# A dynamic convolution followed by a maxout layer: three pairs of taps of columns 24 to 27 added on VectorE, GpSimd's gate as a transfer, sums in three parts, the last copy shared

## The chip, the cores and the metric

The kernel runs on one core of a Trainium2 chip. The metric is the device time of one execution in microseconds, as the median over several executions. In the text TensorE (PE in the profile) does the matrix products, VectorE (DVE) and ScalarE (ACT) the elementwise work, GpSimd (POOL) and SyncE (SP) issue most of the transfers.

## The reference

```python
w = softmax(weight_gen, axis=-1)            # (8, 4160, 8 heads, 7 taps)
x_pad = x with 6 zero rows ahead of each sequence
y[b, s, h, :] = sum over k of w[b, s, h, k] * x_pad[b, s + k, h, :]      # 24 channels a head, 192 in all
g = maximum(y @ w1, y @ w2)                 # 192 -> 1024
out = g @ w_out                             # 1024 -> 192
```

There are 8·4160 = 33280 tokens. The maximum is computed as h1 + relu(h2 − h1): the matrix w2 − w1 makes the "hidden" products, ScalarE applies ReLU to them, and the part h1 @ w_out is the product of y with w1 @ w_out (the tile `w10`).

## The kernel before, in words

**Columns and batches.** Each of the 128 partitions holds 260 consecutive tokens; token c of every partition is "column" c. Columns are worked on in batches of 16 (the last two have 12 and 8). Batches 0 and 1 are split into units of four columns, the others into units of eight. A unit's first column is written (b, o): batch and offset, so (1, 8) holds columns 24 to 27; it is unit 6, counted from 0.

**VectorE per batch.** `mul` (L198, the instruction at L211) multiplies x with the weights for all seven taps, into `m_t`. `adds` (L217) then sums the taps: L227 adds taps 3 to 5 to taps 0 to 2 in one instruction, L233 adds tap 1 to tap 0 and tap 6 to tap 2, L236 adds those two into `y_t`. Between the three additions, `adds` calls a function `beside(i, 3)` for i = 0, 1, 2; it is how other VectorE work is put between them. In the main loop the first half of a batch has there the three parts of `shift` (L177: the logarithm of the sum is subtracted from the weights' exponents), the second half has `red` (L168: the sum over the taps of the exponentials), in two parts, both ahead of L233.

**The softmax on ScalarE.** For batch b the steps are X.b (the exponential, L153), the sums by VectorE (`red`), l.b (the logarithm, L172, one instruction for the whole batch), `shift` on VectorE, and W.b.o (the exponential again, which makes the weights that `mul` takes, L191). Where X, l and W stand in ScalarE's queue of the main loop is given by the table `SOFTMAX_AT`: the key (g, place) is a group of the main loop and a place in it (0: before the group's last ReLU, 1: after the group's results have been copied out). l.5 stands at (16, 1), l.10 at (44, 1). VectorE's work for batches b + 1 to b + 3 is issued by `extra` (L762), called for every tile of batch b; so the sums of batch 5 are issued by the tile with offset 8 of batch 2 and those of batch 10 by the tile with offset 13 of batch 7, which lie in the groups 16 and 44.

**TensorE.** y must be turned for the products. In the opening (units 0 to 7) TensorE does it and adds the taps at the same time: `sum_transpose` (L270, steps y.u; its products at L281) multiplies each tap's block of `m_t` with an identity matrix and accumulates all seven taps in PSUM: 6 blocks · 7 taps · 2 halves = 84 products of 64 columns per unit. From unit 8 on the taps are added on VectorE, and the turned block `yt` comes from a transposing transfer (`transpose`, L241; the transfer at L245 on SyncE's queue).

**The main loop.** A tile is a chunk of hidden products. From group 8 on, a group has three tiles, held in PSUM as `hda`, `hdb`, `hdc`, each with one buffer. In `hidden` (L495) TensorE makes the hidden products of the first two tiles (L336), the first half of the results of earlier columns (`out_first`, L388 and L376, into `op_ps`, one buffer), the third tile's hidden products, and the second half of the results (`out_second`). ScalarE does the three ReLUs (L346) and copies the results out of `op_ps` (`evac`, L434). Before `out_second` TensorE waits for a signal that ScalarE passes on behind the first two ReLUs (`relay`). VectorE's steps of a group (`beside`) are issued before its l step. The tile with number 16 + 3k opens group 8 + k; tile 208 is the first of a unit of batch 13.

**The gate.** `transpose` ends by letting GpSimd copy one column of `yt` into a small tile `gate` (L253). The copy waits for the transposing transfer; the loads of x and of `weight_gen` that GpSimd issues behind it (x for the next batch or the one after it, `weight_gen` for three batches later) start only then.

**The opening.** It is written out as a string of steps, each step being name.arguments: m.b.o is `mul`, n.b `red`, s.b `shift`, y.u `sum_transpose`, e.u the copy of its result into `yt`, h and r hidden products and ReLU, A, B, D, E the parts of the results. The step named `a` calls `adds(b, o, first=True)`, which stops after L227; no step of the string uses it.

**The end.** `evac` has a branch for the very last pair of columns: ScalarE copies both from PSUM into `o_last` (L422), and ScalarE and SyncE issue one transfer each.

Of the kernel before, what the change touches and what calls it, by code (L numbers as in the profile page):

```python
# [9 lines left out]
FP32 = mybir.dt.float32  # L10
BF16 = mybir.dt.bfloat16
# [12 lines left out]
def kernel(  # L24
# [18 lines left out]
    HF = F // 2  # L43
# [8 lines left out]
    NB = len(BATCHES)  # L52
# [27 lines left out]
    consts = ctx.enter_context(tc.tile_pool(name="consts", bufs=1))  # L80
# [83 lines left out]
    def red(b, i=0, of=1):  # L164
        if i == 0:
            s_ts[b] = psm.tile([P, BATCHES[b][1] * H], FP32, name="sum_t", tag="sum")
        hs, at, ap = part(b, i, of)
        nc.vector.reduce_sum(out=s_ts[b][:, hs], in_=_sub(e_ts[b], at, ap), axis=AX.X)  # L168
# [48 lines left out]
    def adds(b, o, first=False, beside=lambda i, of: None):  # L217


        w = dict(pieces(b))[o]  # L220
        n = w * D

        def taps(at, step, cnt):
            return _sub(m_t, K * o * D + at * n, [[step * n, cnt], [1, w * D]])

        beside(0, 3)
        nc.vector.tensor_tensor(out=taps(0, 1, 3), in0=taps(0, 1, 3), in1=taps(3, 1, 3), op=ALU.add)  # L227
        if first:
            return
        beside(1, 3)  # L230
        if b not in y_ts:
            y_ts[b] = py.tile([P, 16 * D], BF16, name="y_t", tag="y")
        nc.vector.tensor_tensor(out=taps(0, 2, 2), in0=taps(0, 2, 2), in1=taps(1, 5, 2), op=ALU.add)  # L233
        beside(2, 3)

        nc.vector.tensor_tensor(  # L236
            out=_sub(y_ts[b], o * D, [[64, 2], [P, 3 * w // 2], [1, 64]]),
            in0=taps(0, 1, 1), in1=taps(2, 1, 1), op=ALU.add,
        )

    def transpose(u):  # L241

        b, o, n = UNITS[u]
        yt = pyt.tile([P, 8 // 2 * 3 * P], BF16, name="yt", tag="yt")
        nc.sync.dma_start_transpose(  # L245
            out=yt[:, 0:n // 2 * 3 * P].rearrange("p (b t) -> p b t", t=P),
            in_=y_ts[b][:, o * D:(o + n) * D],
        )
        yt_ts[u] = yt
        while held:  # L250
            held.pop(0)()

        nc.gpsimd.tensor_copy(out=gate, in_=yt[:, 0:1])  # L253
# [11 lines left out]
        return slice(64 * j, 64 * j + 64)  # L265


    LEFT = (0, 1, 2, K - 1)

    def sum_transpose(u, i=None):  # L270

        b, o, n = UNITS[u]
        assert n == 4
        to = "h" if i == 0 else "o"
        yps = yps_of[u, i] = ps[to].tile([P, 1024], FP32, name="yps", tag="hd" if i == 0 else "op")
        ks = range(6) if i is None else range(3 * i, 3 * i + 3)
        for k in ks:
            for t in range(K):
                at = K * o * D + (t * 6 + k if i is None else (K * i + t) * 3 + k % 3) * P
                for r in range(2):  # L280
                    nc.tensor.matmul(  # L281
                        yps[:, r * 512 + k * 64:r * 512 + (k + 1) * 64],
                        lhsT=m_t[half(r), at:at + P], rhs=ident[half(r), half(r)],
                        start=(k == ks[0] and t == 0), stop=(t == K - 1),
                        skip_group_check=True,
                    )
# [129 lines left out]
    def evac(p, n):  # L416

        tile_, at = op_at[p]
        o = o_t[0]
        if p == NT // 2 - 1:  # L420

            nc.scalar.copy(out=_sub(o_last, 0, [[D, 2], [1, D]]),  # L422
                           in_=_sub(tile_, at, [[512, 2], [1, D]]))
            for j, eng in enumerate((nc.scalar, nc.sync)):
                eng.dma_start(
                    out=bass.AP(tensor=out.tensor, offset=dcol(place(p)[0] + 2 * j) * D, ap=[[CPP * D, P], [1, D]]),
                    in_=o_last[:, j * D:(j + 1) * D],
                )
            return
        runs = [[q for q in range(p, p + n) if column(2 * q)[0] == u]  # L430
                for u in range(column(2 * p)[0], column(2 * (p + n - 1))[0] + 1)]
        for qs in runs:
            c, h = place(qs[0])
            copied = nc.scalar.copy(out=_sub(o, c % 24 * D, [[D, len(qs)], [h * D, 2], [1, D]]),  # L434
                           in_=_sub(tile_, at + (qs[0] - p) * D, [[D, len(qs)], [512, 2], [1, D]]))
# [106 lines left out]
    around = consts.tile([P, 2 * P], BF16, name="around")  # L542
    ident, swap = around[:, 0:P], around[:, 64:64 + P]
    zeros = consts.tile([P, PAD * D], BF16, name="zeros")
    gate = consts.tile([P, 1], FP32, name="gate")
    o_last = consts.tile([P, 2 * D], FP32, name="o_last")

    pstage = ctx.enter_context(ExitStack())
    stage = pstage.enter_context(tc.tile_pool(name="pstage", bufs=1))
# [13 lines left out]
    def load_w(h, wi):  # L563

        wsrc = (moe_w1, moe_w2)[wi]
        return nc.sync.dma_start(
            out=ws["E", wi][:, h * HF:(h + 1) * HF],
            in_=bass.AP(tensor=wsrc.tensor, offset=h * HF, ap=[[F, P], [1, HF]]),
        )

    def load_last(h, wi):

        wsrc = (moe_w1, moe_w2)[wi]
        return nc.sync.dma_start(  # L574
            out=ws["T", wi][half(h), :],
            in_=bass.AP(tensor=wsrc.tensor, offset=P * F + h * HF, ap=[[F, 64], [1, HF]]),
        )
# [124 lines left out]
    def results_buffer(_):  # L702
# [22 lines left out]
        e.0.1 d.0 d.2 t.0 k.3 t.2 T.3 d.1 T.4 h.0 h.1 t.1 X.1 r.0 lx.0.8.4 T.1 lo.0 r.1 m.0.4 n.1 v.0 h.2  # L725
        lx.1.0.8 V.1 y.1 r.2 l.1 h.3 e.1 m.0.8 lg.2@l.1 s.1 V.0 m.0.12 r.3 h.4 W.1.0 m.1.0 y.2 h.5 r.4 p.0
        e.2 r.5 h.6 lx.1.8.8@r.4 lg.3@e.2 y.3 W.1.8 h.7 lh.2 C.1 C.0 C.2 A.3 W.1.4 X.2 r.6 e.3 B.3 m.1.4 h.8
        D.3 y.4 r.7 r.8 Z.0 E.3 n.2 X.3 l.2 m.1.8 A.4 e.4 W.1.12 lx.2.0.8.0@r.7 B.4 h.9 D.4 h.10 r.9 E.4 s.2
        r.10 lg.4@r.9 y.5 W.2.0 A.5 h.11 B.5 h.12 e.5 D.5 n.3 r.11 r.12 A.6 m.1.12 E.5 h.13 B.6 D.6 y.6 r.13
        E.6 h.14 e.6 l.3 lx.2.8.8@r.13 h.15 r.14 A.7 W.2.8 B.7 y.7 D.7 r.15 e.7 E.7  # L730
    """

    make_identity(nc, ident_f)
# [28 lines left out]
    def extra(t):  # L762

        u, k = TILES[t]
        b, o, n = UNITS[u]
        s = o + k

        if s == 0 and b + 1 < NB:
            mul(b + 1, 0)
        later = 0 if b < 4 else 5  # L770
        if s == later and b + 1 < NB:

            c = b + 1
# [51 lines left out]
```

## Time and profile before

| | |
|---|---|
| median of 3 executions | 406.01 us (405.65 to 406.52) |
| the profiled execution | 405.37 us |
| its span, first to last instruction | 403.6 us |
| TensorE's granted clock | 1.00 |
| products of the turning in the opening, L281 | 672, 11.4 us busy |
| L253, the gate | 30, 1332 ns on average |
| L168, the sums | 31, 19.7 us busy |
| L422, the last copy | 1, 479 ns |

A line of the timeline has: start, duration (both us), engine, line of the code, operation, output<-input, shapes, count, and in brackets the idle time of the engine before it and what ended it. In the chain of waits a line has: start, duration, engine, output, line, count. A line of the list of waits has: who waited, for whom, us in total, times, the longest. In the groups, "x27 | 155.4, 5754 | 0.0" means 27 instructions, 155.4 us busy, 5754 ns each, and idle time before them. Consecutive instructions of one engine overlap a little in these records: the next one starts before the one ahead is shown to end.

### The profile page before, as it was taken

Reading aid. Unit: us, or ns where it says so; the run is one execution under the profiler, and the core shown is the slowest. Engines: PE = TensorE matmul, PEld = TensorE weight load, DVE = VectorE, ACT = ScalarE, POOL = GpSimd, SP = SyncE. Lnnn points to the kernel's source line nnn. Section 1 sums busy time; section 2 is a strip of 40 time slices with the busy share of each in tenths; the row PEclk is TensorE's granted clock in tenths of the full one; section 3 lists DMA queues with packets and bytes.
Section 4 is the critical chain, followed back from the end, with each engine's and each line's share of the span. In section 5 each row is a group of like instructions: output and inputs, shape, how many; then the busy total and the mean of one; then the engine's idle time right before and its main releaser. Section 6 shows DMA issues by size and latency. Waiting matters only on the chain.

```text
span 403.6 us, 16321 instructions
## 1 busy us (share of the span) xinstructions
PE 394.8 (98%) x7499; PEld 321.3 (80%) x7499; DVE 369.1 (91%) x211; ACT 360.9 (89%) x466; POOL 72.3 (18%) x96
## 2 busy tenths in 40 slices
PE   7799999999999999999999999999999999999996
PEld 3589999777778777778777778877777877787996
DVE  5999999999999999999999999999999999998200
ACT  5999899999999989999899999989999899888872
POOL 3111031211122210222220122122012121200000
PEclk9999999999999999999999999999999999999999
DMA  8956468767768646864766667777457847558304
GB/s 262 222 140 151 120 124 167 183 164 133 190 110 222 182 79 129 240 187 80 217 187 107 141 192 193 99 215 198 81 115 228 178 80 200 141 106 193 104 31 169
DMA packets 60883, 63.16 MB, mean 157 GB/s; under 512 B 47641, under 2 KB 48665, under 8 KB 60816
## 3 DMA queue, kind: packets, MB, share of 16 engines
q1 hardware_dynamic: 52816, 40.15, 36.4%
q0 software_dynamic: 7856, 21.89, 27.4%
q8 instruction: 58, 0.95, 1.0%
q10 hardware_dynamic: 144, 0.10, 0.1%
q14 instruction: 9, 0.07, 0.1%
HBM read 36.55 MB, written 25.56 MB: 154 GB/s over the span
## 4 chain that ended last, share of the span: by engine, by line
PE 92%; ACT 5%; DMA 1%; SPq 1%; issue 0%
PE op_ps L376 42%; PE hdc L336 13%; PE hdb L336 13%; PE hda L336 13%; PE op_ps L388 8%; ACT rd_t L346 2%; DMA ws0E<-in_moe_w_dram 1%; PE hdp L336 1%; PE yps L281 1%; ACT en_t L191 1%; ACT yt L293 1%; ACT e_t L153 0%; ACT w1t L644 0%; SPq L574 0%; ACT w L622 0%
## 5 line engine op out<-in xcount | busy, mean ns | idle before, releaser
L376 PE MATMUL op_ps<-wo,rd_t 64*128 64x192 bf16 x4160 | 210.6, 243 | 0.0
L376 PEld LDWEIGHTS <-rd_t 64*128 64x128 bf16 x4160 | 181.0, 94 | 14.7
L211 DVE TENSOR_TENSOR m_t<-xb,en_t 128x10752 bf16<-128x10752 bf16 (+2 forms) x39 | 187.8, 4821 | 1.5 <-ACT en_t L191 1.4
L336 PEld LDWEIGHTS <-wd 64*128 64x128 bf16 x1824 | 96.8, 94 | 40.4 <-issue 2.5
L346 ACT ACTIVATE rd_t<-hdc 128x1024 bf16<-128x1024 f32 x82 | 84.1, 1025 | 17.8 <-PE hdc L336 16.2
L253 POOL CAST gate<-yt 128x1 f32<-128x1 bf16 x30 | 39.9, 1332 | 271.3 <-DMA yt<-y_t 271.3
L346 ACT ACTIVATE rd_t<-hda 128x1024 bf16<-128x1024 f32 x81 | 83.4, 1030 | 0.2 <-ACT o_t L434 0.2
L346 ACT ACTIVATE rd_t<-hdb 128x1024 bf16<-128x1024 f32 x81 | 83.5, 1031 | 0.0
L227 DVE TENSOR_TENSOR m_t<-m_t 128x4608 bf16<-128x4608 bf16 (+1 forms) x30 | 73.0, 2433 | 0.1
L336 PE MATMUL hdc<-yt,wd 64*128 64x512 bf16 (+1 forms) x552 | 67.9, 353 | 0.0
L434 ACT COPY o_t<-op_ps 128x384 f32<-128x384 f32 (+1 forms) x99 | 56.1, 577 | 12.4 <-PE op_ps L376 12.3
L336 PE MATMUL hdb<-yt,wd 64*128 64x512 bf16 (+1 forms) x540 | 67.1, 355 | 0.0
L336 PE MATMUL hda<-yt,wd 64*128 64x512 bf16 (+1 forms) x540 | 67.1, 355 | 0.0
L388 PE MATMUL op_ps<-w,yt 64*128 64x192 bf16 x780 | 55.5, 243 | 0.0
L388 PEld LDWEIGHTS <-yt 64*128 64x128 bf16 x780 | 39.0, 94 | 14.5 <-issue 0.3
L233 DVE TENSOR_TENSOR m_t<-m_t 128x3072 bf16<-128x3072 bf16 (+1 forms) x30 | 50.2, 1674 | 0.1
L191 ACT ACTIVATE en_t<-wg_t 128x896 bf16<-128x896 f32 (+3 forms) x48 | 35.7, 773 | 3.0 <-PE op_ps L376 2.0
L236 DVE TENSOR_TENSOR y_t<-m_t 128x1536 bf16<-128x1536 bf16 (+1 forms) x30 | 27.5, 916 | 0.6
L177 DVE TENSOR_TENSOR wg_t<-wg_t,sum_t 128x280 f32<-128x280 f32 (+6 forms) x46 | 22.2, 483 | 0.0
L168 DVE TENSOR_REDUCE sum_t<-e_t 128x64 f32<-128x448 f32 (+3 forms) x31 | 19.7, 639 | 2.3 <-ACT e_t L153 2.3
L125 POOL DMA_DIRECT2D xb<-in_x_dram x34 | 18.2, 537 | 17.3 <-ACT rd_t L346 11.0
L153 ACT ACTIVATE e_t<-wg_t 128x896 f32<-128x896 f32 (+2 forms) x18 | 15.9, 886 | 2.1 <-DMA wg_t<-in_weight_gen_dram 2.1
(40 smaller groups left out, 110.0 us busy)
## 6 DMA issues: line engine op xcount, KB each, us to landing
out_dram<-o_t SPq DMA_DIRECT2D x21, 768.0 KB, 4.3
xb<-in_x_dram POOLq DMA_DIRECT2D x30, 384.0 KB, 5.0
out_dram<-o_t SPq DMA_DIRECT2D x22, 384.0 KB, 3.7
wg_t<-in_weight_gen_dram POOLq DMA_DIRECT2D x13, 448.0 KB, 5.7
xb<-xb POOLq DMA_DIRECT2D x7, 288.0 KB, 5.1
wg_t<-in_weight_gen_dram SPq DMA_DIRECT2D x2, 448.0 KB, 5.2
xb<-in_x_dram POOLq DMA_DIRECT2D x4, 192.0 KB, 6.4
xs<-in_x_dram SPq DMA_DIRECT2D x1, 576.0 KB, 4.3
```

Source lines behind the costliest of these rows:

```text
L177: nc.vector.tensor_tensor(out=w_t, in0=w_t, in1=_sub(s_ts[b], hs.start, [[1, hs.stop - hs.start], [0, K]]), op=ALU.subtract)
L191: act = nc.scalar.activation(out=_sub(en_ts[b], (o * WGC + ((i or 0) * J + j) * N * K) * 2, [[2 * N, K], [2, N], [1, 2]]), in_=_sub(wg_ts[ ...
L211: return nc.vector.tensor_tensor(out=m_out, in0=x_in, in1=_sub(en_ts[b], at * H * 2, [[2, K * n * H], [0, G // 2], [1, 2]]), op=ALU.mult,)
L227: nc.vector.tensor_tensor(out=taps(0, 1, 3), in0=taps(0, 1, 3), in1=taps(3, 1, 3), op=ALU.add)
L233: nc.vector.tensor_tensor(out=taps(0, 2, 2), in0=taps(0, 2, 2), in1=taps(1, 5, 2), op=ALU.add)
L236: nc.vector.tensor_tensor(out=_sub(y_ts[b], o * D, [[64, 2], [P, 3 * w // 2], [1, 64]]), in0=taps(0, 1, 1), in1=taps(2, 1, 1), op=ALU.add,)
L253: nc.gpsimd.tensor_copy(out=gate, in_=yt[:, 0:1])
L336: nc.tensor.matmul(hid_out(t, f, j), lhsT=wd_at(j, s, f // 4, f % 4 * P, P), rhs=_sub(yt_ts[u][half(j), :], (s + j) % 3 * P, [[3 * P, w // ...
L346: relu_of[t0] = nc.scalar.activation(out=rd[:, k * 1024:(k + n) * 1024], in_=hd[:, at:at + n * 1024], func=AF.Relu)
L376: return nc.tensor.matmul(op_out(c), lhsT=rd[rows, k * 1024 + at:k * 1024 + at + P], rhs=wo[rows, f * D:(f + 1) * D], start=False, stop=(r ...
L388: nc.tensor.matmul(op_out(c + j), lhsT=yt_ts[u][half(j), (3 * i + (s + j) % 3) * P:(3 * i + (s + j) % 3 + 1) * P], rhs=w10[half(j), s * D: ...
L434: copied = nc.scalar.copy(out=_sub(o, c % 24 * D, [[D, len(qs)], [h * D, 2], [1, D]]), in_=_sub(tile_, at + (qs[0] - p) * D, [[D, len(qs)] ...
```

## The change

- The opening gets the step a.1.8 behind m.1.8: VectorE adds taps 3 to 5 of unit (1, 8) to its taps 0 to 2. `sum_transpose` then accumulates four taps for this unit (0, 1, 2 and 6) where it took seven.
- The gate is a transfer of two elements, issued by GpSimd, where it was a copy by GpSimd.
- `red` in the second half of a batch comes in three parts, the third between L233 and L236.
- The last pair of columns is copied by ScalarE and VectorE, one column each, into two tiles; ScalarE and SyncE issue the transfers as before.
- `load_w` and `load_last` get a case and an argument that no step uses.

```diff
         nc.vector.tensor_tensor(out=taps(0, 1, 3), in0=taps(0, 1, 3), in1=taps(3, 1, 3), op=ALU.add)
         if first:
+            fewer.add((b, o))
             return
...
-        nc.gpsimd.tensor_copy(out=gate, in_=yt[:, 0:1])
+        nc.gpsimd.dma_start(out=gate, in_=yt[0:1, 0:2])
...
-    LEFT = (0, 1, 2, K - 1)
+    fewer = set()
...
+        taps = (0, 1, 2, K - 1) if (b, o) in fewer else range(K)
         for k in ks:
-            for t in range(K):
+            for t in taps:
...
-            nc.scalar.copy(out=_sub(o_last, 0, [[D, 2], [1, D]]),
-                           in_=_sub(tile_, at, [[512, 2], [1, D]]))
-            for j, eng in enumerate((nc.scalar, nc.sync)):
+            for j, (eng, copy) in enumerate(((nc.scalar, nc.scalar.copy), (nc.sync, nc.vector.tensor_copy))):
+                copy(out=o_last[j], in_=tile_[:, at + 512 * j:at + 512 * j + D])
                 eng.dma_start(
                     out=bass.AP(tensor=out.tensor, offset=dcol(place(p)[0] + 2 * j) * D, ap=[[CPP * D, P], [1, D]]),
-                    in_=o_last[:, j * D:(j + 1) * D],
+                    in_=o_last[j],
                 )
...
-    gate = consts.tile([P, 1], FP32, name="gate")
-    o_last = consts.tile([P, 2 * D], FP32, name="o_last")
+    gate = consts.tile([1, 2], BF16, name="gate")
+    o_last = [consts.tile([P, D], FP32, name=f"o_last{j}") for j in range(2)]
...
-        D.3 y.4 r.7 r.8 Z.0 E.3 n.2 X.3 l.2 m.1.8 A.4 e.4 W.1.12 lx.2.0.8.0@r.7 B.4 h.9 D.4 h.10 r.9 E.4 s.2
+        D.3 y.4 r.7 r.8 Z.0 E.3 n.2 X.3 l.2 m.1.8 a.1.8 A.4 e.4 W.1.12 lx.2.0.8.0@r.7 B.4 h.9 D.4 h.10 r.9
+        E.4 s.2 ...
...
-            adds(b + 1, 8, beside=lambda i, of: red(b + 3, i, 2) if b + 3 < NB and i < 2 else None)
+            adds(b + 1, 8, beside=lambda i, of: red(b + 3, i, 3) if b + 3 < NB else None)
```

More of the change, by code (lines that the diff above doesn't have):

```diff
@@ L565, in load_w, with load_last @@
         wsrc = (moe_w1, moe_w2)[wi]
+        at, w = (0, F) if h == 2 else (h * HF, HF)
         return nc.sync.dma_start(
-            out=ws["E", wi][:, h * HF:(h + 1) * HF],
-            in_=bass.AP(tensor=wsrc.tensor, offset=h * HF, ap=[[F, P], [1, HF]]),
+            out=ws["E", wi][:, at:at + w],
+            in_=bass.AP(tensor=wsrc.tensor, offset=at, ap=[[F, P], [1, w]]),
         )
-    def load_last(h, wi):
+    def load_last(h, wi, act=0):
         wsrc = (moe_w1, moe_w2)[wi]
-        return nc.sync.dma_start(
+        return (nc.scalar if act else nc.sync).dma_start(
             out=ws["T", wi][half(h), :],
@@ L727 @@
         e.2 r.5 h.6 lx.1.8.8@r.4 lg.3@e.2 y.3 W.1.8 h.7 lh.2 C.1 C.0 C.2 A.3 W.1.4 X.2 r.6 e.3 B.3 m.1.4 h.8
-        D.3 y.4 r.7 r.8 Z.0 E.3 n.2 X.3 l.2 m.1.8 A.4 e.4 W.1.12 lx.2.0.8.0@r.7 B.4 h.9 D.4 h.10 r.9 E.4 s.2
-        r.10 lg.4@r.9 y.5 W.2.0 A.5 h.11 B.5 h.12 e.5 D.5 n.3 r.11 r.12 A.6 m.1.12 E.5 h.13 B.6 D.6 y.6 r.13
-        E.6 h.14 e.6 l.3 lx.2.8.8@r.13 h.15 r.14 A.7 W.2.8 B.7 y.7 D.7 r.15 e.7 E.7
+        D.3 y.4 r.7 r.8 Z.0 E.3 n.2 X.3 l.2 m.1.8 a.1.8 A.4 e.4 W.1.12 lx.2.0.8.0@r.7 B.4 h.9 D.4 h.10 r.9
+        E.4 s.2 r.10 lg.4@r.9 y.5 W.2.0 A.5 h.11 B.5 h.12 e.5 D.5 n.3 r.11 r.12 A.6 m.1.12 E.5 h.13 B.6 D.6
+        y.6 r.13 E.6 h.14 e.6 l.3 lx.2.8.8@r.13 h.15 r.14 A.7 W.2.8 B.7 y.7 D.7 r.15 e.7 E.7
     """
```

## The prediction

> **What bounds the kernel now.** I read the page first, then the chain of waits, then the timeline engine by engine, and last each place where ScalarE or TensorE takes something that VectorE has made.
>
> ```profile
> span 403.6 us, 16321 instructions
> PE 394.8 (98%) x7499; PEld 321.3 (80%) x7499; DVE 369.1 (91%) x211; ACT 360.9 (89%) x466; POOL 72.3 (18%) x96
> ...
> 41.97 1.22 PE yps L281 x84
> 43.19 1.31 PE hdp L336 x24
> ```
>
> The profiled execution took 405.37 us, 1.8 more than its span, against a median of 406.01; I work out a difference on the span and add it to the median. TensorE is the bound: it is busy 98% of the span, and its pieces of the chain follow without a gap (the products at 41.97 end at 43.19, where the next begin). A microsecond taken from TensorE is therefore won, as long as ScalarE and VectorE can be earlier too. VectorE is the one to doubt:
>
> ```profile
> 31.32 2.95 DVE L211 TENSOR_TENSOR m_t<-xb,en_t 128x5376 bf16<-128x5376 bf16 x1
> 34.19 1.08 DVE L177 TENSOR_TENSOR wg_t<-wg_t,sum_t 128x896 f32<-128x896 f32 x1
> ...
> DVE m_t L211 <- ACT en_t L191: 1.4, 1, 1.4
> ```
>
> The third line is VectorE's only wait after the opening (the list of waits has it once, at 364 us). Between 34 and 357 us VectorE runs without a pause, so whatever is put in at 34 us moves everything behind it by the full amount.
>
> **The columns 24 to 27.** The four remaining taps need 6·4·2 = 48 products where seven needed 84. The 84 took 1.22 us, so the 36 that go are worth 36/84·1.22 = **0.52 us of TensorE**. Nothing hides them; but the gain lasts only while nobody makes TensorE wait later.
>
> On VectorE the new addition is of 128x2304 elements and stands behind the multiplication m.1.8 whose result it reads. The same two forms, in the same dependence, stand near the end:
>
> ```profile
> 357.13 2.96 DVE L211 TENSOR_TENSOR m_t<-xb,en_t 128x5376 bf16<-128x5376 bf16 x1
> 360.12 1.36 DVE L227 TENSOR_TENSOR m_t<-m_t 128x2304 bf16<-128x2304 bf16 x1
> ...
> 36.90 1.09 ACT L191 ACTIVATE en_t<-wg_t 128x896 bf16<-128x896 f32 x1
> ```
>
> There the addition began 2.99 us after the multiplication; before, the next instruction (independent) began 34.19 − 31.32 = 2.87 after it. So a.1.8 begins at 34.31, and an independent successor begins about 0.08 before the end of 1.36 (as 34.19 lies 0.08 before 31.32 + 2.95), at 35.59: **VectorE is 1.40 us later from there on** (1.28 without the dependence, at least). The first taker, the weights W.2.0 on ScalarE (36.90), needs s.2, which then ends at 35.59 + 1.08 = 36.67: covered, by 0.2 us (without that cover ScalarE would be late by the difference, less than what l.5 brings below). The products of y.6 at 41.97 have over 6 us.
>
> **The sums in three parts.** What each part costs is read from the starts:
>
> ```profile
> 80.20 0.61 DVE L168 TENSOR_REDUCE sum_t<-e_t 128x64 f32<-128x448 f32 x1
> 80.73 2.55 DVE L227 TENSOR_TENSOR m_t<-m_t 128x4608 bf16<-128x4608 bf16 x1
> 83.20 0.62 DVE L168 TENSOR_REDUCE sum_t<-e_t 128x64 f32<-128x448 f32 x1
> 83.72 1.75 DVE L233 TENSOR_TENSOR m_t<-m_t 128x3072 bf16<-128x3072 bf16 x1
> 85.51 0.96 DVE L236 TENSOR_TENSOR y_t<-m_t 128x1536 bf16<-128x1536 bf16 x1
> ...
> 95.24 1.75 DVE L233 TENSOR_TENSOR m_t<-m_t 128x3072 bf16<-128x3072 bf16 x1
> 96.91 0.50 DVE L177 TENSOR_TENSOR wg_t<-wg_t,sum_t 128x336 f32<-128x336 f32 x1
> ...
> 316.87 0.50 DVE L168 TENSOR_REDUCE sum_t<-e_t 128x48 f32<-128x336 f32 x1
> 317.28 2.56 DVE L227 TENSOR_TENSOR m_t<-m_t 128x4608 bf16<-128x4608 bf16 x1
> ```
>
> A sum over 448 elements takes 0.53 from start to start, over 336 it takes 0.41; so 280 take 0.35. L236 waits for L233 and begins 1.79 behind it, but an instruction that is independent begins 1.67 behind (96.91). The third sum therefore fills 0.12 us that were empty. Two parts: 0.53 + 0.53 + 1.79 = 2.85; three parts (280, 280, 336): 0.35 + 0.35 + 1.67 + 0.41 = 2.78. That is **0.07 us less per batch**, 0.9 over 13 batches, off a VectorE that doesn't set the end. [...]
>
> What counts is when the sums are complete. The logarithm l.5 of batch 5 reads all of them, and the last third now comes behind L233, the second addition. In the block above: 80.20 + 0.35 + 2.47 (L227) + 0.35 + 1.67 = 85.04, and 0.50 for itself: 85.54, where now it is 83.82. With VectorE's delay at this place, 1.40 less the 0.07 that batch 4 has saved, it is **86.87**. And l.5 isn't moved:
>
> ```profile
> 83.94 0.80 ACT L434 COPY o_t<-op_ps 128x768 f32<-128x768 f32 x1
> 84.64 0.31 ACT L172 ACTIVATE sum_t<-sum_t 128x128 f32<-128x128 f32 x1
> 84.85 1.02 ACT L346 ACTIVATE rd_t<-hda 128x1024 bf16<-128x1024 f32 x1
> 85.75 1.03 ACT L346 ACTIVATE rd_t<-hdb 128x1024 bf16<-128x1024 f32 x1
> 86.75 1.02 ACT L346 ACTIVATE rd_t<-hdc 128x1024 bf16<-128x1024 f32 x1
> 87.67 0.47 ACT L434 COPY o_t<-op_ps 128x384 f32<-128x384 f32 x1
> ...
> 87.19 0.83 PE L336 MATMUL hda<-yt,wd 64*128 64x512 bf16 x6
> ...
> 88.48 0.43 PE L388 MATMUL op_ps<-w,yt 64*128 64x192 bf16 x6
> ```
>
> How fast such a signal is, the opening shows:
>
> ```profile
> 4.72 1.15 DVE L168 TENSOR_REDUCE sum_t<-e_t 128x64 f32<-128x448 f32 x2 [2.28 <-ACT e_t L153]
> ...
> 5.38 0.26 ACT L172 ACTIVATE sum_t<-sum_t 128x64 f32<-128x64 f32 x1 [0.22 <-DVE sum_t L168]
> ```
>
> The first sum (0.62) ends at 5.34, the logarithm begins 0.04 later. So ScalarE would reach l.5 at 84.64 − 0.52 = 84.12 and stand until 86.91: a wait of 2.8 us that doesn't exist now. Queued behind it are the three ReLUs and the copy of group 17. From the start of l.5: 0.21 to the first ReLU, 0.91, 0.91 and 0.92 to the copy, 0.47 for the copy, 0.05 to release TensorE: 3.47 us, so 90.38. TensorE needs that copy at 88.48, since op_ps has one buffer in this phase. It begins at 90.38, **1.90 us later than before**. The other takers are less late: the hidden products at 87.19 need the first ReLU, ready at 88.2, so 1.0. The 0.52 gained are swallowed in this wait, as VectorE, not TensorE, sets when l.5 runs.
>
> The same pattern comes once more at l.10:
>
> ```profile
> 198.53 0.61 DVE L168 TENSOR_REDUCE sum_t<-e_t 128x64 f32<-128x448 f32 x1
> ...
> 203.25 0.31 ACT L172 ACTIVATE sum_t<-sum_t 128x128 f32<-128x128 f32 x1
> ...
> 207.14 0.43 PE L388 MATMUL op_ps<-w,yt 64*128 64x192 bf16 x6
> ```
>
> The sums end at 198.53 + 5.34 + 1.40 − 6·0.07 = 204.85. By itself this would cost 204.89 + 3.47 − 207.14 = 1.22 us. But ScalarE is 1.90 later by then and reaches l.10 at 205.15: no wait. VectorE runs on its own clock, so such delays do not add; the largest counts.
>
> **The gate.** Now the gate's copy waits out VectorE's multiplication:
>
> ```profile
> 74.53 5.75 DVE L211 TENSOR_TENSOR m_t<-xb,en_t 128x10752 bf16<-128x10752 bf16 x1
> 78.60 1.73 POOL L253 CAST gate<-yt 128x1 f32<-128x1 bf16 x1 [8.96 <-DMA yt<-y_t]
> 80.27 0.53 POOL L125 DMA_DIRECT2D xb<-in_x_dram  x1
> ...
> L211 DVE TENSOR_TENSOR m_t<-xb,en_t 128x10752 bf16<-128x10752 bf16 x27 | 155.4, 5754 | 0.0
> ```
>
> It lasts until the multiplication ends. A transfer in its place costs GpSimd one issue, 0.53 like the row below it; at worst it stays at 1.73. The loads behind it start 1.2 us earlier at this place, and are used a batch (24 us) later: 0 on the path either way. VectorE gains nothing: with the copy waiting beside it this multiplication took 5.75 us, as the 27 of its form did on average.
>
> **The last copy.** One ScalarE copy of 384 elements becomes two of 192, side by side.
>
> ```profile
> L434 ACT COPY o_t<-op_ps 128x384 f32<-128x384 f32 x69 | 31.9, 478 | 3.5 <-PE op_ps L376 3.5
> ...
> L434 ACT COPY o_t<-op_ps 128x768 f32<-128x768 f32 x30 | 24.1, 805 | 8.9 <-PE op_ps L376 8.9
> ```
>
> (805 − 478)/384 = 0.85 ns an element, so 192 take 478 − 163 = 315 ns: **−0.16 us**, fully at the end. VectorE's copy out of PSUM isn't in the trace; VectorE is idle there, and between 0.2 and 0.4 us for it the gain is 0.08 to 0.16.
>
> **Sum:** +1.90 − 0.16 = +1.74; 406.01 + 1.74 = **407.7 us**. With the delay at 1.28 instead of 1.40, or 0.25 more in ScalarE's string, +1.6 to +2.0.
>
> **Rivals.**
> *The wait is hidden.* If TensorE can do without ScalarE for the time of the wait, it keeps its 0.52 and the end its 0.16: −0.7, 405.3 us. For it: now the sums end at 83.82, l.5 begins 0.82 later, and the copy that TensorE needs at 88.48 ends at 88.14; both places have room. It decides if the sums end by 84.45 (84.49 + 3.47 is 88.48 − 0.52); even with no delay of VectorE's the third part would end at 85.54. 12%.
> *The delays add.* If ScalarE's stand makes VectorE late as well (by its weights), l.10 costs its 1.22 + 0.52 again: +3.5, 409.5 us. The point is where weights come later than the multiplication that takes them. Against it: the list has VectorE waiting for ScalarE's weights just once, at the end. 12%.
> *A turned block becomes the limit instead.* With l.5 harmless, the next thinnest place is the block of tile 208:
>
> ```profile
> 316.04 0.96 POOL L253 CAST gate<-yt 128x1 f32<-128x1 bf16 x1 [9.85 <-DMA yt<-y_t]
> ...
> 317.49 0.83 PE L336 MATMUL hda<-yt,wd 64*128 64x512 bf16 x6
> ```
>
> It has landed 1.45 us ahead of its use; TensorE 0.52 earlier and VectorE 0.6 later leave 0.3. A landing 0.6 us slower would take half of the gain: 405.7 us. 6%.
>
> **How the numbers follow.** The forecast has 70%, by itself 407.2 to 408.4. Slower by over 0.2% (0.8 us, about what a measurement of this kernel can tell from no change): forecast and adding delays, 82%. The hidden wait lies at −0.17%, so its 12% are split, 5 faster and 7 same; with the 6 of the block that is 13% same. The range runs from 405.9 to 408.9: it leaves out the hidden wait and half of the adding one, 18%.
>
> **What would show it.** The list of waits must have ScalarE's sum_t waiting for VectorE's sum_t once for some 2.8 us, at 84 us, and no second time over 0.3; TensorE must have about 2.4 us of gaps between 86 and 91 and none after; y.6 must take 0.70; VectorE's shift s.2 must begin at 35.6. I am wrong if ScalarE passes l.5 without that wait, or if it waits and TensorE runs on.

## The result, and the profile after

| | before | after |
|---|---|---|
| median (range), 6 executions each | 405.70 us (405.50 to 406.52) | 407.25 us (407.01 to 407.83) |
| ratio after / before, with its interval | | 1.0042 [1.0030, 1.0054] |
| the profiled execution, its span | 405.37 us, 403.6 us | 407.56 us, 405.8 us |

The change makes the kernel about 1.6 us slower. In the profile after, lines behind the edits have moved by one or two: `op_ps` is now L378 and L390 (they were L376 and L388), the hidden products are L338 (L336), `evac` is L435 (L434), the gate L254 (L253), the additions L234 and L237 (L233 and L236). First the head of the page and the rows that answer to the opening:

```profile
span 405.8 us, 16275 instructions
```

```profile
31.71 2.95 DVE L211 TENSOR_TENSOR m_t<-xb,en_t 128x5376 bf16<-128x5376 bf16 x1
...
34.69 1.36 DVE L227 TENSOR_TENSOR m_t<-m_t 128x2304 bf16<-128x2304 bf16 x1
...
35.97 1.08 DVE L177 TENSOR_TENSOR wg_t<-wg_t,sum_t 128x896 f32<-128x896 f32 x1
...
42.17 0.88 PE L283 MATMUL yps<-around,m_t 64*128 64x64 bf16 x48
42.87 1.49 PE L338 MATMUL hdp<-yt,wd 64*128 64x256 bf16 x24
```

The multiplication m.1.8 starts at 31.71, 0.39 later than before (31.32), though nothing ahead of it was changed; other profiled executions start earlier or later too, so where a time of this profile is held against one of before, the 0.39 is named or taken off. The shift that began 34.19 − 31.32 = 2.87 us behind m.1.8 now begins 4.26 behind it: VectorE is 1.39 us later. The products of y.6 take 42.87 − 42.17 = 0.70 us instead of 1.22.

The timeline where batch 5's sums are completed, VectorE and ScalarE, then TensorE:

```profile
81.92 0.43 DVE L168 TENSOR_REDUCE sum_t<-e_t 128x40 f32<-128x280 f32 x1
...
82.27 2.54 DVE L227 TENSOR_TENSOR m_t<-m_t 128x4608 bf16<-128x4608 bf16 x1
...
84.74 0.43 DVE L168 TENSOR_REDUCE sum_t<-e_t 128x40 f32<-128x280 f32 x1
...
85.09 1.75 DVE L234 TENSOR_TENSOR m_t<-m_t 128x3072 bf16<-128x3072 bf16 x1
...
86.76 0.49 DVE L168 TENSOR_REDUCE sum_t<-e_t 128x48 f32<-128x336 f32 x1
87.17 0.94 DVE L237 TENSOR_TENSOR y_t<-m_t 128x1536 bf16<-128x1536 bf16 x1
87.28 0.31 ACT L172 ACTIVATE sum_t<-sum_t 128x128 f32<-128x128 f32 x1 [2.68 <-DVE sum_t L168]
...
90.21 0.49 ACT L435 COPY o_t<-op_ps 128x384 f32<-128x384 f32 x1
```

```profile
85.75 0.83 PE L338 MATMUL hdc<-yt,wd 64*128 64x512 bf16 x6
...
87.47 0.83 PE L378 MATMUL op_ps<-wo,rd_t 64*128 64x192 bf16 x16 [0.90 <-ACTq L411]
...
88.55 0.82 PE L338 MATMUL hda<-yt,wd 64*128 64x512 bf16 x6 [0.25 <-ACT rd_t L348]
...
89.47 0.82 PE L338 MATMUL hdb<-yt,wd 64*128 64x512 bf16 x6
...
90.75 0.42 PE L390 MATMUL op_ps<-w,yt 64*128 64x192 bf16 x6 [0.46 <-ACT o_t L435]
```

ScalarE stands for 2.68 us until VectorE's third sum has ended at 87.25. TensorE is 0.13 us earlier than before when it reaches this place (85.75 against 85.88: the late opening and the 0.52 gained) and 2.27 us later when it leaves it (90.75 against 88.48): 2.40 us lost between five neighbouring steps, at four stops. The first stop, at 87.47, waits for the relay (the `ACTq L411` in the bracket), which stands behind l.5 in ScalarE's queue. The brackets show less, since the rows of products overlap (before, a row of 0.83 us where the next begins 0.65 behind it); starts are the safer reading: before, these steps came 0.65, 0.66, 0.65 and 0.64 us apart, now 1.72, 1.08, 0.92 and 1.28. From there to the end TensorE loses and wins nothing more: its last products begin 2.26 us later (400.12 against 397.86), and the span is 405.8 − 403.6 = 2.2 us longer.

The list of waits has ScalarE waiting for a sum once more, for 0.2 us, and nothing else of the kind:

```profile
DVE o_last L425 <- ACT o_last L425: 24.1, 1, 24.1
...
DVE m_t L211 <- ACT en_t L191: 3.0, 2, 2.8
...
ACT sum_t L172 <- DVE sum_t L168: 2.9, 2, 2.7
```

The second line is VectorE waiting for ScalarE's weights. That wait, at 364 us before, has grown from 1.4 to 2.8 us, because ScalarE is later there by more than VectorE is; no product of TensorE is later for it. The first line is the tail, which didn't go as forecast:

```profile
401.70 0.48 ACT L435 COPY o_t<-op_ps 128x384 f32<-128x384 f32 x1 [0.82 <-PE op_ps L378]
402.31 0.32 ACT L425 COPY o_last<-op_ps 128x192 f32<-128x192 f32 x1
...
402.66 0.36 DVE L425 COPY o_last<-op_ps 128x192 f32<-128x192 f32 x1 [24.14 <-ACT o_last L425]
403.05 0.34 SPq L426 DMA_DIRECT2D out_dram<-o_last  x1
```

VectorE's half of the last copy waits for ScalarE's half and starts when that has ended. Both read the same PSUM tile, `op_ps`, in which TensorE has summed the products.

### The profile page after: what moved, and what is told of

The parts are those of the page before. It is cut to its first block, busy times and chain, and to the rows that moved or that the text cites. A ratio compares the mean times of both kernels' runs of the same rounds, so it can differ in the third digit from the quotient of the medians.

```text
span 405.8 us, 16275 instructions
## 1 busy us (share of the span) xinstructions
PE 395.7 (98%) x7463; PEld 320.4 (79%) x7463; DVE 370.3 (91%) x226; ACT 360.6 (89%) x466; POOL 49.2 (12%) x96
## 4 chain that ended last, share of the span: by engine, by line
PE 79%; DVE 13%; ACT 5%; DMA 1%; issue 1%; SPq 0%; DVEq 0%; ACTq 0%
PE op_ps L378 37%; PE hdc L338 11%; PE hdb L338 11%; PE hda L338 11%; PE op_ps L390 7%; DVE m_t L211 6%; DVE m_t L227 2%; ACT rd_t L348 2%; DVE m_t L234 2%; DMA xs<-in_x_dram 1%; PE yps L283 1%; DVE y_t L237 1%; DVE sum_t L168 1%; PE hdp L338 1%; DVE wg_t L177 0%
## 5 line engine op out<-in xcount | busy, mean ns | idle before, releaser
L378 PE MATMUL op_ps<-wo,rd_t 64*128 64x192 bf16 x4160 | 210.5, 243 | 0.9 <-ACTq L411 0.9
L378 PEld LDWEIGHTS <-rd_t 64*128 64x128 bf16 x4160 | 180.7, 94 | 16.0 <-ACTq L411 1.4
L211 DVE TENSOR_TENSOR m_t<-xb,en_t 128x10752 bf16<-128x10752 bf16 (+2 forms) x39 | 187.5, 4814 | 3.0 <-ACT en_t L191 3.0
L338 PEld LDWEIGHTS <-wd 64*128 64x128 bf16 x1824 | 96.4, 94 | 41.1 <-issue 2.9
L227 DVE TENSOR_TENSOR m_t<-m_t 128x4608 bf16<-128x4608 bf16 (+1 forms) x31 | 74.1, 2392 | 0.1
L338 PE MATMUL hdc<-yt,wd 64*128 64x512 bf16 (+1 forms) x552 | 67.9, 353 | 0.0
L338 PE MATMUL hda<-yt,wd 64*128 64x512 bf16 (+1 forms) x540 | 67.0, 355 | 0.2 <-ACT rd_t L348 0.2
L435 ACT COPY o_t<-op_ps 128x384 f32<-128x384 f32 (+1 forms) x99 | 56.1, 578 | 12.4 <-PE op_ps L378 12.4
L338 PE MATMUL hdb<-yt,wd 64*128 64x512 bf16 (+1 forms) x540 | 67.0, 355 | 0.1
L390 PE MATMUL op_ps<-w,yt 64*128 64x192 bf16 x780 | 55.5, 243 | 0.5 <-ACT o_t L435 0.5
L254 POOL DMA_DIRECT2D gate<-yt x30 | 15.3, 512 | 298.9 <-DMA yt<-y_t 298.9
L390 PEld LDWEIGHTS <-yt 64*128 64x128 bf16 x780 | 38.8, 94 | 15.3 <-issue 1.0
L234 DVE TENSOR_TENSOR m_t<-m_t 128x3072 bf16<-128x3072 bf16 (+1 forms) x30 | 50.0, 1667 | 0.1
L237 DVE TENSOR_TENSOR y_t<-m_t 128x1536 bf16<-128x1536 bf16 (+1 forms) x30 | 27.2, 906 | 0.1
L168 DVE TENSOR_REDUCE sum_t<-e_t 128x40 f32<-128x280 f32 (+6 forms) x44 | 21.3, 486 | 2.3 <-ACT e_t L153 2.3
```

The lines of the kernel that those rows point to most:

```text
L211: return nc.vector.tensor_tensor(out=m_out, in0=x_in, in1=_sub(en_ts[b], at * H * 2, [[2, K * n * H], [0, G // 2], [1, 2]]), op=ALU.mult,)
L237: nc.vector.tensor_tensor(out=_sub(y_ts[b], o * D, [[64, 2], [P, 3 * w // 2], [1, 64]]), in0=taps(0, 1, 1), in1=taps(2, 1, 1), op=ALU.add,)
L338: nc.tensor.matmul(hid_out(t, f, j), lhsT=wd_at(j, s, f // 4, f % 4 * P, P), rhs=_sub(yt_ts[u][half(j), :], (s + j) % 3 * P, [[3 * P, w // ...
L378: return nc.tensor.matmul(op_out(c), lhsT=rd[rows, k * 1024 + at:k * 1024 + at + P], rhs=wo[rows, f * D:(f + 1) * D], start=False, stop=(r ...
L390: nc.tensor.matmul(op_out(c + j), lhsT=yt_ts[u][half(j), (3 * i + (s + j) % 3) * P:(3 * i + (s + j) % 3 + 1) * P], rhs=w10[half(j), s * D: ...
```

## The experiments

Every ratio is against the kernel before, run on the same chip in the same rounds.

| what was run | median, before | ratio, interval |
|---|---|---|
| three taps alone | 406.06, 405.52 | 1.0015 [1.0003, 1.0026] |
| after, sums in two parts | 406.08, 405.52 | 1.0018 [1.0007, 1.0030] |
| after, l.5 later | 406.55, 405.52 | 1.0033 [1.0020, 1.0047] |
| after, five l steps later | 405.09, 405.52 | 0.9988 [0.9978, 0.9998] |
| the same, last pair in two PSUM tiles | 405.12, 405.77 | 0.9984 [0.9975, 0.9993] |
| the same, one last copy | 405.66, 405.71 | 1.0010 [0.9990, 1.0030] |
| the same, gate as a copy | 409.08, 405.71 | 1.0091 [1.0066, 1.0115] |
| gate as a transfer alone | 405.75, 405.77 | 0.9999 [0.9982, 1.0017] |
| sums in three parts alone | 409.20, 405.77 | 1.0092 [1.0067, 1.0116] |
| sums in three parts, gate as a transfer | 406.18, 405.71 | 1.0007 [0.9996, 1.0017] |
| five l steps later, taps of (1, 12) too | 406.56, 405.77 | 1.0017 [0.9997, 1.0036] |

**The wait taken away.** If the loss is ScalarE standing at l.5, putting the logarithms behind the sums must bring the 0.52 us back.

```diff
 SOFTMAX_AT
-(16, 1): "l.5"   (34, 0): "l.8"   (44, 1): "l.10"   (56, 0): "l.12"   (72, 0): "l.15"
+(18, 0): "l.5"   (34, 1): "l.8"   (46, 0): "l.10"   (56, 1): "l.12"   (73, 0): "l.15"
```

> All parts of the change are kept, but the five logarithms that stand close behind their sums are moved to later places of ScalarE's queue: l.5 from (16, 1) to (18, 0), l.8 from (34, 0) to (34, 1), l.10 from (44, 1) to (46, 0), l.12 from (56, 0) to (56, 1), l.15 from (72, 0) to (73, 0). The theory (ScalarE stands at l.5 until the third sum is there, and that is the whole loss): no wait of ScalarE for a sum after the opening, no gap of TensorE between 80 and 300 us, TensorE 0.5 us earlier than in the kernel before; time 1.9 + 0.5 = 2.4 us below the changed kernel's, so 404.8 to 405.3. Rival one (VectorE's delay costs TensorE through the turned blocks): gaps of TensorE at the tiles 200 to 240, waiting for a turned block; time 405.7 or above. Rival two (gate or last copy cost the time): still 407.

It took 405.09 us, inside the theory's range: 2.2 less than after, 0.43 less than before (0.1 to 0.9 by the interval). TensorE runs through the place without a stop:

```profile
85.29 0.83 PE L338 MATMUL hdc<-yt,wd 64*128 64x512 bf16 x6
...
87.89 0.43 PE L390 MATMUL op_ps<-w,yt 64*128 64x192 bf16 x6
...
89.34 0.31 ACT L172 ACTIVATE sum_t<-sum_t 128x128 f32<-128x128 f32 x1
```

From `hdc` to L390 it is 2.60 us, as before the change. Not all of the 0.52 arrives. The third rival's place, the block of tile 208, now stops TensorE; here the version with later l steps, then before:

```profile
315.58 0.83 PE L338 MATMUL hdc<-yt,wd 64*128 64x512 bf16 x6
...
317.27 0.82 PE L338 MATMUL hda<-yt,wd 64*128 64x512 bf16 x6 [0.20 <-DMA yt<-y_t]
```

```profile
316.18 0.83 PE L336 MATMUL hdc<-yt,wd 64*128 64x512 bf16 x6
```

From `hdc` to the first product of tile 208 it is 1.69 us, before it was 317.49 − 316.18 = 1.31. So in this profile 0.38 of the 0.52 is lost again here, and 0.14 is kept.

**l.5 alone.** Only the first row of that edit, `(16, 1): "l.5"` to `(18, 0): "l.5"`.

> Of the changed kernel only l.5 is moved, from (16, 1) to (18, 0); l.10 stays at (44, 1). The theory (VectorE runs on its own clock, so each place has a bound of its own and the largest counts): no gap at 86 us, but now one at 205 to 209 us, where ScalarE waits 204.89 - (203.25 - 0.52) = 2.2 us at l.10 and TensorE ends 1.22 us later than before: time 406.8 to 407. Rival (delays add, each place costs its own): in the changed kernel l.10 would already have cost something, so moving l.5 alone would win the full 2.4 us: 404.9.

406.55 us. The expected 406.8 to 407 was counted from 406.01; against before it is 1.0 more, where 0.8 to 1.0 was expected. The wait has gone to l.10, where the prediction had put its bound of 1.22 us:

```profile
205.07 0.31 ACT L172 ACTIVATE sum_t<-sum_t 128x128 f32<-128x128 f32 x1 [2.07 <-DVE sum_t L168]
```

TensorE loses 1.75 us there, the 1.22 and the 0.52 (L390 at 208.53 against 207.14; it was 0.36 ahead). In the kernel after there is no wait at l.10. So the two delays don't add; the larger covers the smaller.

**The shares of taps and sums.** First the taps alone: the kernel before with a.1.8 and the four taps; then after with the old two sums.

```diff
-        for k in ks:
-            for t in range(K):
+        taps = (0, 1, 2, K - 1) if (b, o) in fewer else range(K)
+        for k in ks:
+            for t in taps:
...
-... l.2 m.1.8 A.4 ...
+... l.2 m.1.8 a.1.8 A.4 ...
```

> The kernel before with only the tap addition a.1.8 and the four taps in the turning of columns 24 to 27; old gate, old sums, old last copy. Theory: the same as with two parts, TensorE 0.25 us later than before at l.5, so 405.9 to 406.1 and within 0.3 of the run with two parts, because gate and last copy are worth nothing. Rival (the gain on TensorE is won): 0.52 below before, 405.2.

```diff
-adds(b + 1, 8, beside=lambda i, of: red(b + 3, i, 3) if b + 3 < NB else None)
+adds(b + 1, 8, beside=lambda i, of: red(b + 3, i, 2) if b + 3 < NB and i < 2 else None)
```

> The changed kernel with the sums in two parts again. Theory: the sums of batch 5 end at 83.82 + 1.40 = 85.22, l.5 begins at 85.26 where ScalarE would reach it at 84.12: a wait of 1.1 us, and TensorE is 85.26 + 3.47 - 88.48 = 0.25 us later than before, instead of 1.90: time 405.9 to 406.1. If the delay of VectorE by the tap addition alone made the loss: 407.2 as with three parts.

The taps alone make ScalarE wait 1.02 us at l.5 (the line below), and the kernel after with two sums shows the same 1.02:

```profile
85.36 0.31 ACT L172 ACTIVATE sum_t<-sum_t 128x128 f32<-128x128 f32 x1 [1.02 <-DVE sum_t L168]
```

Both took 406.1 us, as expected, 0.5 to 0.6 over before. In both profiles TensorE loses 0.75 us at l.5 (the 0.52 and some 0.23 more, where 0.25 was expected) and then some at the block of tile 208: 0.41 with the taps alone (318.24 − 316.52 against 1.31) and 0.13 with two sums (319.50 − 318.06). Against after, the third part of the sums is worth about 1.0 us by the ratios (1.0042 and 1.0018); at l.5 it makes the difference between a wait of 1.02 us and one of 2.68.

**The gate alone.**

```diff
-        nc.gpsimd.tensor_copy(out=gate, in_=yt[:, 0:1])
+        nc.gpsimd.dma_start(out=gate, in_=yt[0:1, 0:2])
```

> The kernel before with only the gate as a transfer. Theory: GpSimd 0.51 us per gate instead of 1.33, loads earlier, nothing on the path: the same as before within 0.3 us, and VectorE's large multiplication still 5.75 us. Rival (earlier loads collide with the transposing transfers): blocks land later and TensorE waits at the tiles 208 to 240, 0.5 us or more above before.

No change, and GpSimd's busy time falls from 72.3 to 49.2 us, as the 30 gates go from 1332 to 512 ns; the multiplications of L211 still take 4819 ns on average (before 4821). So far "0" was right.

**The sums alone.** The kernel before with the sums in three parts (the line of `adds` above, the other way round), the gate still a copy.

> The kernel before with only the sums in three parts. Theory: no delay of VectorE, but the last third of batch 5 ends at 85.54 instead of 83.82, l.5 begins at 85.58 (ScalarE there at 84.64: a wait of 0.9 us), TensorE is 85.58 + 3.47 - 88.48 = 0.57 us later; at l.10 the sums end at 203.45, 0.2 us after ScalarE is there, which the delay of 0.57 covers. Time 0.4 to 0.7 above before. Rival (the third part fills a gap of VectorE and is free, so the loss is due to the tap addition alone): the same as before, within 0.2 us.

It took 409.2 us, 3.4 over before: a miss. The wait at l.5 is as small as expected (0.76 us, 0.55 for TensorE), but the groups of the page show GpSimd's copy of one column at three times the mean of before:

```profile
L253 POOL CAST gate<-yt 128x1 f32<-128x1 bf16 x30 | 126.1, 4203 | 189.2 <-DMA yt<-y_t 189.2
```

One of them, with what VectorE did meanwhile (two views of one window):

```profile
114.65 13.11 POOL L253 CAST gate<-yt 128x1 f32<-128x1 bf16 x1 [9.30 <-DMA yt<-y_t]
127.70 0.53 POOL L125 DMA_DIRECT2D xb<-in_x_dram  x1
```

```profile
110.14 5.76 DVE L211 TENSOR_TENSOR m_t<-xb,en_t 128x10752 bf16<-128x10752 bf16 x1
115.81 0.45 DVE L177 TENSOR_TENSOR wg_t<-wg_t,sum_t 128x280 f32<-128x280 f32 x1
...
121.95 5.76 DVE L211 TENSOR_TENSOR m_t<-xb,en_t 128x10752 bf16<-128x10752 bf16 x1
127.62 0.44 DVE L168 TENSOR_REDUCE sum_t<-e_t 128x40 f32<-128x280 f32 x1
```

The copy waits through the rest of a multiplication, three shifts and three additions in turn, and a second multiplication, all instructions with two inputs, and ends when the first reduction has begun (127.76, the reduction began at 127.62). Eight of the 30 copies are like this, 10.3 to 13.6 us each, where before none was over 1.85. That VectorE's two-input instructions hold the copy is read from these rows. Those of before alone don't show it: there 13 of the 30 copies got in at the end of a multiplication with a shift, also of two inputs, behind it. Why eight copies lose so often stays open.

Loads queued behind a held copy come late, the one at 127.70 by 11.4 us (with the gate as a transfer, below, it is issued at 116.27). Behind the opening VectorE's multiplication waits for them four times, 1.39, 0.20, 0.97 and 9.13 us; this is the first (the bracket names ScalarE, which had long been done):

```profile
135.22 5.76 DVE L211 TENSOR_TENSOR m_t<-xb,en_t 128x10752 bf16<-128x10752 bf16 x1 [1.39 <-ACT o_t L434]
```

A late VectorE then does what the added taps did: the sums of batches 10 and 15 come late, and ScalarE stands at l.10 and at l.15:

```profile
205.28 0.31 ACT L172 ACTIVATE sum_t<-sum_t 128x128 f32<-128x128 f32 x1 [1.38 <-DVE sum_t L168]
...
324.39 0.28 ACT L172 ACTIVATE sum_t<-sum_t 128x96 f32<-128x96 f32 x1 [2.44 <-DVE sum_t L168]
```

These two cost TensorE 1.05 and 0.93 us (its L388 behind l.10 begins 1.60 later than before, 208.75 against 207.14, the one behind l.15 2.53 later, 326.38 against 323.86). The longest of VectorE's waits is at the last batch:

```profile
352.08 10.30 POOL L253 CAST gate<-yt 128x1 f32<-128x1 bf16 x1 [9.10 <-DMA yt<-y_t]
362.32 0.53 POOL L125 DMA_DIRECT2D xb<-in_x_dram  x1
...
369.91 0.57 POOL L145 DMA_DIRECT2D xb<-zeros  x1 [6.52 <-DMA xb<-in_x_dram]
...
374.44 2.96 DVE L211 TENSOR_TENSOR m_t<-xb,en_t 128x5376 bf16<-128x5376 bf16 x1 [9.13 <-ACT rd_t L346]
```

The last x is issued at 362.32, the zeros that follow it at 369.91, and VectorE's multiplication of the last batch stands for 9.13 us. (The bracket names ScalarE as the releaser, which had long been done; the late transfer of zeros is what fits: the multiplication begins 4.5 us behind its issue, and in a version below, where the zeros are issued as late, the bracket names them.) These 9.13 us cost TensorE only another 0.38 in this profile (389.15 against 386.25 is 2.90). The profiled execution took 408.28 us, 0.9 less than the median, so the shares can differ in others.

**The sums in three parts with the gate as a transfer.** This tells whether the late loads come from the copy or from the sums themselves: the two edits above together; the added taps and the shared last copy are left out. (The "five taps" of the text below are the seven that TensorE adds before.)

> The kernel before, with the sums in three parts and the gate as a transfer; five taps for every block and the old last copy stay. Theory: the sums in three parts alone cost 409.2 because GpSimd's copy was held up by VectorE's unbroken run of two-input instructions and the loads behind it came 10 to 13 us late; as a transfer the gate does not read through GpSimd's engine, so every gate is issued within 1.5 us of its rows, no VectorE row waits for a load after the first 60 us, and what is left is the wait at l.5 (0.76 us of ScalarE at about 85 us, some 0.3 to 0.6 us of the end): 406.0 to 406.5. Rival: the late loads come from the sums in three parts themselves (the order of VectorE's instructions, or the buffers' release) and not from the copy: 408 or more with the same waits for a load.

406.18 us, inside the theory's 406.0 to 406.5; the rival's 408 is out. Behind the opening no VectorE row waits for a load, and ScalarE doesn't stand at l.10. The same place as above, of this kernel:

```profile
115.77 0.51 POOL L253 DMA_DIRECT2D gate<-yt  x1 [11.31 <-DMA yt<-y_t]
116.27 0.55 POOL L125 DMA_DIRECT2D xb<-in_x_dram  x1
```

The load that was issued at 127.70 is issued at 116.27. What is left is the wait at l.5, 0.77 us in this profile.

**The same, from the other side.** The version with five later l steps, its gate a copy again.

> The kernel after with l.5, l.8, l.10, l.12 and l.15 put later (the version that took 405.1), but the gate as GpSimd's copy of one column again. Theory: with the sums in three parts VectorE's shifts run without a gap between two-input instructions, so some of the 30 copies take 10 to 13 us instead of 1.3, their loads land late and VectorE waits for them: GpSimd's busy time over 120 us, 407.5 to 410. Rival: the gate is worth nothing once the l-steps stand later, because the moved steps or the three added taps shift the copies to other instructions: 405.0 to 405.5, no copy over 2 us.

409.08 us, 4.0 more than with the transfer. Eleven of the 30 copies take 10.3 to 13.3 us, and VectorE again waits longest for the last load:

```profile
375.28 2.96 DVE L211 TENSOR_TENSOR m_t<-xb,en_t 128x5376 bf16<-128x5376 bf16 x1 [9.60 <-DMA xb<-zeros]
```

Here the bracket names the transfer itself. In this profile, of an execution of 410.94 us, this wait does cost: TensorE stops twice for blocks turned too late (384.31 and 391.80), 3.6 of the 5.8 us that it loses. The rest falls on two late loads of `weight_gen`, for which ScalarE waits, and on tile 208. So the gate as a transfer is worth nothing in the kernel before and 3 to 4 us once the sums come in three parts.

**The last copy.** The version with later l steps, once with ScalarE's single copy of both columns, once with the last pair in two PSUM tiles, so that neither half has to wait for the other.

```diff
-copy(out=o_last[j], in_=tile_[:, at + 512 * j:at + 512 * j + D])
+nc.scalar.copy(out=_sub(o_last, 0, [[D, 2], [1, D]]), in_=_sub(tile_, at, [[512, 2], [1, D]]))
```

> The version that took 405.1 (the kernel after with five l-steps later), but the last pair of columns copied by ScalarE in one instruction as before. Theory: the shared copy is worth nothing, since in the kernel after its halves run one behind the other (0.32 and 0.36 us) and end no earlier than one copy of both: within 0.15 us of the 405.1 version, the last two issues 0.5 to 0.6 us behind TensorE's end instead of 0.7 to 0.8. Rival: the shared copy is worth the 0.16 us that was forecast, or more: 405.3 or over.

```diff
-            out_room(now, ("r", "a", "c")[i])
+            if now[0] // 2 == NT // 2 - 1:
+                op_at[now[0] // 2] = tuple(ps[k].tile([P, 1024], FP32, name="op_" + k, tag=k) for k in "cb"), 0
+            else:
+                out_room(now, ("r", "a", "c")[i])
...
-copy(out=o_last[j], in_=tile_[:, at + 512 * j:at + 512 * j + D])
+copy(out=o_last[j], in_=tile_[j][:, 0:D])
```

> As the run with the later logarithms, and the last pair of columns has two PSUM tiles, one for each column, so that VectorE's copy waits for TensorE alone. Theory (the two copies ran one after the other, 0.32 and 0.36 us, because both read one tile): they now begin together, the last transfer is issued 0.35 us sooner after TensorE's last product, and the time is 0.2 to 0.35 below the run with the later logarithms: 404.8. Rival (the end is set by the transfer's landing, not by the copies): no difference.

The times don't separate them: 405.66 (405.00 to 409.33) with one copy, 405.12 with two tiles, 405.09 with halves in turn. The tails show more. With one copy, then with two tiles:

```profile
399.78 0.48 ACT L436 COPY o_t<-op_ps 128x384 f32<-128x384 f32 x1 [0.82 <-PE op_ps L378]
...
400.90 0.34 SPq L427 DMA_DIRECT2D out_dram<-o_last  x1
```

```profile
399.59 0.48 ACT L437 COPY o_t<-op_ps 128x384 f32<-128x384 f32 x1 [0.82 <-PE op_ps L380]
...
400.20 0.36 DVE L427 COPY o_last<-op_b 128x192 f32<-128x192 f32 x1 [23.79 <-PE op_c L380]
400.23 0.32 ACT L427 COPY o_last<-op_c 128x192 f32<-128x192 f32 x1 [0.16 <-PE op_c L380]
400.58 0.38 ACTq L428 DMA_DIRECT2D out_dram<-o_last  x1
```

Counted from the start of the copy ahead (the 384 elements of `o_t`), the last issue stands at 1.12 us with one copy, at 1.35 with halves in turn (403.05 − 401.70), at 0.99 with two tiles. The view of the transfers gives the time from issue to landing as the last number, here of the last transfer with halves in turn and then with two tiles (with one copy the later of the two took 2.0):

```profile
out_dram<-o_last SPq DMA_DIRECT2D x1, 96.0 KB, 1.8
```

```profile
out_dram<-o_last SPq DMA_DIRECT2D x1, 96.0 KB, 2.1
```

So the last landing is at 3.12 with one copy, 3.15 with halves in turn and 3.09 with two tiles: the same within what these rows, one execution each, can show. With two tiles the copies do run side by side (starts 0.03 apart), and the expected 0.2 to 0.35 us isn't there.

**More of the same addition.** The later l steps let VectorE be later; do the taps of the next unit pay as well?

```diff
-... A.6 m.1.12 E.5 ...
+... A.6 m.1.12 a.1.12 E.5 ...
```

> As the run with the later logarithms, and the three pairs of taps of columns 28 to 31 are added on VectorE too (a.1.12 behind m.1.12), so that TensorE loses another 36 products (0.52 us) and VectorE is another 1.4 us later. Theory (with the logarithms out of the way VectorE's delay reaches TensorE through the turned blocks, whose slack at tile 208 is used up already): TensorE waits for a block at tile 208 and is there about 1.4 us later than with one addition: 406.2 to 406.6. Rival (blocks have room left): another 0.5 us won, 404.6.

406.56 us, 1.4 to 1.5 more than without: the time was as expected, the place wasn't. The second 0.52 is mostly gone at once: TensorE waits for a ReLU at 48.26 (1.11 us behind the step ahead, before 0.66). Then its weight loads wait for turned blocks, three times by the list of waits:

```profile
PEld L338 <- DMA yt<-y_t: 1.4, 3, 0.7
```

The longest two are at 284.95 (tile 184) and 366.15 (tile 240), 0.7 us each by the starts; tile 208, the expected place, has none. At six units from tile 184 on the gate, which waits for the turned block, begins only after the first product that takes it. Behind l.5 and l.10 the turned block is the next limit, and a later VectorE makes it later. The best version is thus the one with five later l steps, 0.1 to 0.2% under before, with or without the two PSUM tiles.

## Why the prediction was right, point by point

**VectorE later by 1.40.** Measured 1.39. The addition began 2.98 us behind its multiplication (2.99 was taken from the far end of the trace) and the successor 1.28 behind it.

**0.52 us of TensorE, lost again.** y.6 takes 0.70. That the gain was real and was swallowed at l.5 is shown by the version with later logarithms: in its profile TensorE is 0.52 us ahead (0.59 with the earlier opening) up to tile 208, where 0.38 goes; the medians differ by 0.43.

**The sums.** The starts in the block above are 0.35, 2.47, 0.35, 1.67 and 0.41 apart, each as forecast from other places of the trace before. They have a fixed part in them: 0.53 us for 448 elements (before) and 0.41 and 0.35 for 336 and 280 (after) give, as an estimate from these three, 1.07 ns an element and 0.05 us for each reduction. So the third part costs VectorE 0.05, and the block is 0.07 shorter only because 0.12 of it now fills the time in which L237 waits for L234. The last sum ends at 87.25; 86.87 plus the late opening of 0.39 is 87.26.

**The wait at l.5.** Forecast 2.8, measured 2.68. The string from l.5 to the copy's release was 3.47 us, and 87.28 + 3.47 is 90.75, where L390 begins: 1.88 later than before without the opening, against 1.90. What I didn't name is where TensorE stops first: not at `op_ps` but 90.75 − 87.47 = 3.28 us earlier, at the signal that ScalarE relays ahead of `out_second`. That signal lies on the same string, so the sum at its end was the same.

**l.10.** No wait in after, and 2.07 us of it when l.5 is out of the way, as "the largest counts" has it. The rival of adding delays falls with this; the hidden wait fell at l.5.

**The last copy.** This term failed: −0.16 was forecast and nothing is there. I took the two halves to run side by side because they stand on two engines; they read one tile, and VectorE's (0.36 us, for which the trace before had no row) waited for ScalarE's. Besides, in the three profiles of the tail an earlier last issue doesn't bring an earlier last landing. Without this term the sum is +1.90 instead of +1.74. Measured is 1.55 between the medians (1.2 to 2.2 by the interval of the ratio), and 1.87 at TensorE's last products in the profiles (2.26 less the 0.39 of the opening). That the sum with the wrong term is the closer one to the medians is luck; they don't resolve 0.16 us.

**The gate.** "0 on the path either way" holds for the edit by itself and is wrong for it as part of this change. I priced the copy at what it took before, 1.33 us, and didn't ask what the sums in three parts do to it. With them, the copy costs 3 to 4 us; in the profile of the sums alone 2.0 of the 2.4 us that come behind l.5 fall at l.10, a place that the prediction names, and at l.15, which it doesn't. It didn't show in the time because the change brought the remedy along with the illness.

**The turned block.** Its place, tile 208, was right, and the chance of 6% was for it as the limit of this kernel, which it isn't. With l.5 harmless it takes 0.38 us of TensorE in the profile, more than the half of 0.52 that was its price. (The range from 405.9 leaves out this rival's 405.7 too, so by its own numbers 24% and not 18%.)

## What to carry to other kernels

An instruction added to an engine that never pauses makes everything behind it late by its whole length (here an addition of 1.36 us made VectorE 1.39 later), so list the consumers that stand at a fixed place in another engine's queue, work out each one's slack, and move them with it. Splitting work so that it fills gaps also moves its last piece; what reads all pieces counts from the last (here l.5 waited 1.02 us with two sums, 2.68 with three). Price every edit against the kernel with the other edits in it: one that is worth nothing alone can be what makes another affordable (here the gate as a transfer, 405.75 against 405.77 alone, and 406.18 against 409.20 once the sums came in three parts).

## What the runs showed of the hardware

- A GpSimd copy of one column was held for up to 13.6 us beside VectorE's two-input instructions in a row (8 of 30 copies with the sums alone, 10.3 to 13.6 us; 11 of 30 with later l steps and the gate as a copy, 10.3 to 13.3). Of the 8, 7 ended when a multiplication had ended and a reduction began; the last one ended at 362.38, where a multiplication ended at 362.34 and the addition that reads its result began at 362.37. Why other copies get in sooner stays open: before, the copy at 114.50 ended at 115.85, at the end of a multiplication with the same shift behind it. A transfer issued in the copy's place took 0.50 to 0.52 us each time, beside the same instructions.
- Before, VectorE's L236, which reads the result of the L233 ahead, began 0.04 us behind its end (1.79 from start to start); a shift, which doesn't, began 0.08 ahead of the end of such an L233 (1.67). The 0.12 between them is room for a small independent instruction: after, the third sum begins 1.67 behind its L234.
- In the version with later l steps, the transposing transfer for tile 208 took 5.3 us from issue to landing, where the median of the 30 is 4.0. A packet of the queue that the view of the transfers calls `instruction` moved in that time, and from 315.5 to 316.5 the queues moved only 4 to 9 GB/s. Over the 60 transposing transfers of before and after, all 14 that took over 4.1 us had such a packet in their time; the 25 that had none took 2.8 to 4.0. That goes together; it wasn't tried whether one makes the other.
- The opening varies from one profiled execution to the next: m.1.8 begins at 31.25 with later l steps, at 31.32 before, at 31.39 with the sums alone, at 31.45 with the taps alone, at 31.49 with l.5 alone and at 31.71 after. With two sums, where VectorE waited 1.9 us for the first x (before 0.5), the reduction ahead of it begins only at 32.00 (before 30.33).
